# Moving six weight pieces out of attention, four splits from GpSimd to VectorE, and some routing steps, in a three-stage kernel

## The chip, the cores and the metric

The kernel runs on one core of a Trainium2 chip. The metric is the device time of one execution in microseconds (us); lower is better. The engines are called as in the profile: PE is TensorE (matmuls), PEld its weight loads, DVE is VectorE, ACT is ScalarE, POOL is GpSimd, SP is SyncE, which here issues nearly all DMAs.

## The reference

Three stages follow each other on 1536 tokens (2 batches of 768) of 512 values (8 heads of 64).

```python
# 1. attention: keys near the query, and one summary of each block of 32
k_sum, v_sum = k.reshape(.., nb, 32, D).max(3), v.reshape(.., nb, 32, D).mean(3)
a = softmax([where(abs(i - j) < 16, scale * q @ k.T, -1e9), scale * q @ k_sum.T + log(32)])
x = a @ [v, v_sum]                                   # then [1536, 512]
# 2. routed experts: 8 of them, 192 tokens each; pairs (token, expert) are served
#    in the order of falling logits, a full expert takes no more
order = argsort(-(x @ w_gate).flatten())
for tok, e in order:
    if assigned[tok] < 0 and counts[e] < 192:
        assigned[tok] = e
x = relu(x @ w1[e]) @ w2[e]                          # e = assigned[token]
# 3. mixture: every token through 4 domains, 512 -> 1024 -> 512
p = domain_probs / domain_probs.sum(-1)
out = sum(p[:, e] * (relu(x @ v1[e]) @ v2[e]) for e in range(4))
```

The weights are float32. Every large product is made of three half-precision ones: each weight (and each activation) is split into a high half and the rest that the high half leaves.

## The kernel before

**Attention** runs over 24 steps of 128 queries, software-pipelined; `ORDER` lists what a step issues, in the order in which the engines get it. During the later steps `router.first` counts, chunk by chunk, which tokens each expert would take (DVE operations at L521 to L546 of the router, small PE products at L529, L556 and L565). SP's queue carries the loads `kq`, `vb`, `vn` of attention and, between them, weight pieces.

**Weight pieces.** A piece is 128 x 512 float32 (256 KB). It lands in one of a few rotating buffers (`raw`, later also `more`) and is split by `split(hi, lo, r)`: `hi` is the float16 copy, `lo` the difference in bfloat16. `Feed` keeps the pieces in one list: `until(key)` splits all pieces up to a key, `pump` issues as many loads as buffers are free, `next` splits the one that is next if its place is free. Who splits depends on `phase` and on the piece: the first ones of attention are split whole by POOL (L787 and L788), later ones have `hi` on ACT (L790) and `lo` on POOL (L791), and the first four pieces of each routed expert have `lo` on DVE (also L791).

**Pieces within attention.** `hook(i)` is called once in each step and splits the pieces whose entry in the table `HOOK` is this step. Pieces numbered below `POOLHI` go whole to POOL. All 16 pieces of domain 0 and of domain 1 are taken so (32 entries, `w20dt` and `w21dt` in the rows). Pieces of domain 2 (`w2k`, `w2v`) come behind attention: four of them (`NEXT`), then the 16 of the first routed expert (`wp`), then its other twelve, then domain 3 (`w23dt`), then the experts 1 to 7.

**Experts and mixture.** `expert(p)` gives nine jobs: `start` (gathered rows `xg`, which POOL's indirect DMAs at L916 bring, are turned on PE and split by ACT and DVE into `xeh` and `xel`), four `up` jobs (they give `heh`, `hel`) and four `down` jobs (`y0h`, `y0l`). `mixture(t0, nt)` takes `nt` row tiles of 128 tokens through the four domains (`hmh`, `hml`, then `po` and `acc`). `PLAN` says which experts' jobs are slipped into which mixture: expert 0 runs first and alone, expert 1 beside mixture tile 0, experts 2 and 3 beside tiles 1 and 2, experts 4 and 5 beside tiles 3 to 5, experts 6 and 7 beside tiles 6 to 8.

**Routing.** `Router.phases` decides for one expert after another which tokens it takes. It is a generator, a ping-pong of short DVE operations and small PE products (`rt`); each `yield r` names about how long its step takes. A model clock sets where the steps stand in the program: `spend(us)` moves it on by the planned PE work, and `advance` issues the next step and sets when the one behind it is due:

```python
        clock[1] = max(clock[:2]) + SLOW * r + HOP
```

The order on every engine is thus fixed when the program is built; an engine that comes to an instruction whose input is not there waits, and all behind it wait too.

Of the kernel before, what the change touches and what calls it, by code (L numbers as in the profile page):

```python
# [15 lines left out]
OP = mybir.AluOpType  # L16
# [26 lines left out]
class Feed:  # L43
# [16 lines left out]
    def next(self, free):  # L60

        self.pump()
        if self.used in self.held and self.clock[0] >= self.since[self.used] + 3.0 and free(self.used):
            self.jobs[self.used][1](self.held.pop(self.used))
            self.used += 1
            self.pump()
# [10 lines left out]
def three(nc, o, a, b, first, last):  # L77

    for n, (i, j) in enumerate(((0, 0), (0, 1), (1, 0))):
# [8 lines left out]
PLAN = [(0, 1, [1], 26.0, 0.0), (1, 2, [2, 3], 3.0, 7.4), (3, 3, [4, 5], 14.0, 10.6),  # L90
        (6, 3, [6, 7], 2.5, 4.1), (9, 3, [], 0.0, 1.0)]
WB = 5
FEED = [0.96, 0.71, 365.54]
HOOK = [5, 8, 9, 10, 11, 12, 13, 14, 16, 17, 18, 18, 19, 19, 20, 20, 21, 21, 22, 22, 23, 23, 24, 24, 25, 25, 26, 26,
        27, 27, 28, 28]

SOON, NEXT = 0, 4
SCHED = {"prep": [1, 1, 2, 2, 3, 4, 4, 5], "sum": 8, "v": 9, "store": 10, "spread": 11, "kq0": 4, "kq1": 7, "vn": 6}
ORDER = [("pv", 3), ("at", 2), ("r1", 5), ("x", 3), ("r2", 5), ("xt3", 4), ("x2", 3), ("r5", 6), ("at2", 2),
         ("prep", 0), ("r6", 6), ("r3", 5), ("score", 0), ("logit", 4), ("l", 4), ("r0", 4), ("r7", 4), ("r8", 4),  # L100
# [641 lines left out]
def attention_moe_mixture_kernel(  # L742
# [13 lines left out]
    nc = tc.nc  # L756
# [24 lines left out]
    phase = [0]  # L781
    zero = cst.tile([128, 1], F32, name="zero")
    nc.gpsimd.memset(zero, 0.0)

    def split(hi, lo, r, eng=None):
        if phase[0] == 0:
            nc.gpsimd.tensor_tensor(hi, r, zero.to_broadcast([128, PW]), op=OP.add)  # L787
            nc.gpsimd.tensor_tensor(lo, r, hi, op=OP.subtract)  # L788
        else:
            nc.scalar.activation(hi, r, AF.Copy)  # L790
            (eng or nc.gpsimd).tensor_tensor(lo, r, hi, op=OP.subtract)  # L791

    W2 = {}
    feed = Feed(RAW - 1)
# [9 lines left out]
    def add_w2(e, home, js):  # L804

        def load(i):
            r = raw_piece()
            h, c = divmod(i, KD)
            nc.sync.dma_start(r, moe2_w1[e, c * 128:(c + 1) * 128, h * PW:(h + 1) * PW] if h < F // PW
                              else moe2_w2[e, (i - KF) * 128:(i - KF + 1) * 128])  # L810
            return r

        def use(i, r):
            W2[e, i] = home(i)
            split(*W2[e, i], r)

        for i in js:
            feed.add(("w2", e, i), lambda i=i: load(i), lambda r, i=i: use(i, r), lambda: True)

    def kept(pool, e):  # L820
        t = [pool.tile([128, 2 * KF, PW], d, name=f"w2{e}{d}") for d in (F16, BF)]
        return lambda i: [x[:, i] for x in t]

    def reused():

        held = {}

        def part(s, i):
            n = 8 if s == 0 and i >= 8 else 4
            if (s, i // n, n) not in held:  # L830
                d = (F16, BF)[s]
                held[s, i // n, n] = (lod.tile([128, 8, PW], d, name="w2v", tag="vn") if n == 8 else
                                      lod.tile([128, 4, PW], d, name="w2k", tag="kq", bufs=6))
            return held[s, i // n, n][:, i % n]

        return lambda i: [part(s, i) for s in range(2)]

    add_w2(0, kept(cst, 0), range(16))
    add_w2(1, kept(cst, 1), range(16))
    home2 = reused()  # L840
    add_w2(2, home2, range(SOON))

    def hook(i):
        if i == 2:
# [35 lines left out]
        for j in js:  # L880
            feed.add(("p", p, j), lambda j=j: load_piece(p, j), lambda r, j=j: use_piece(p, j, r), lambda: p in EREG)

    add_w2(2, home2, range(SOON, SOON + NEXT))
    add_routed(0, range(16))
    add_w2(2, home2, range(SOON + NEXT, 16))
    add_w2(3, kept(mcst, 3), range(16))
    for p in range(1, E):
        add_routed(p, range(16))
# [35 lines left out]
    def advance():  # L924
        r = next(route, None)
        if r is None:
            clock[1] = 1e9
            return
        if isinstance(r, tuple):
            known[0], r = r  # L930
            when[known[0]] = clock[0]
        clock[1] = max(clock[:2]) + SLOW * r + HOP

    def need(p):
        while known[0] < p:
# [18 lines left out]
    def expert(p):  # L954

        y = [t[:, :, (p % 2) * CAP:(p % 2 + 1) * CAP] for t in YB[p // 2 % 2]]

        def start():
            need(p)
            ready(p, 3)  # L960
            for half in range(2):
                t, p0, n, s0 = place(p, half)
                xg = XG[p, half][p0:p0 + n]
                px = ps.tile([128, KD, 128], F32, name="mm", bufs=3)
                for c in range(KD):
                    nc.tensor.transpose(px[:, c, :n], xg[:, c * 128:(c + 1) * 128], identf[p0:p0 + n, p0:p0 + n])
                parts([x[:, :, s0:s0 + n] for x in XE], px[:, :, :n], SX)
                nc.vector.tensor_copy(PD[p0:p0 + n, t], xg[:, DM:ROW])
            taken.add(p)

        def up(j):
            ready(p, 2 * j + 1)
            ph = ps.tile([128, 2, CAP], F32, name="mm", bufs=3)
            for f in range(2):
                w = [t.rearrange("x (c f) -> x c f", c=KD) for t in WP[p, 2 * j + f]]
                for c in range(KD):
                    three(nc, ph[:, f], [t[:, c] for t in w], [x[:, c] for x in XE], f == 0 and c == 0, c == KD - 1)
            relu([h[:, 2 * j:2 * j + 2] for h in HE], ph)
            eaten[0] += 2

        def down(j):
            ready(p, 2 * j + 9)
            py = ps.tile([128, CAP], F32, name="mm", bufs=3)
            for f in range(KF):
                w = [t[:, f % KD * 128:(f % KD + 1) * 128] for t in WP[p, KF + 2 * j + f // KD]]
                three(nc, py, w, [h[:, f] for h in HE], f == 0, f == KF - 1)
            parts([t[:, j] for t in y], py, SY / SX)
            eaten[0] += 2

        def steady():  # L990
            return known[0] >= p and clock[0] >= when[p] + LATE and feed.used > feed.at["p", p, 3]

        return ([(start, steady)]
                + [(lambda j=j: up(j), lambda: True) for j in range(4)]
                + [(lambda j=j: down(j), lambda: True) for j in range(4)])
# [63 lines left out]
    def spend(us):  # L1059
        clock[0] += us  # L1060
        while clock[2] < clock[0]:
            clock[2] += FEED[clock[0] > FEED[2]]
            feed.next(place_for)
        while clock[1] <= clock[0]:
            advance()

    need(0)
    feed.until(("w2", 2, SOON + NEXT - 1))
    clock[1] = 0.0
    for _ in range(EARLY):  # L1070
        advance()
    for f, _ in expert(0):
        f()
        spend(2.0)
    for t0, nt, side, at, gap in PLAN:
        jobs = [f for p in side for f in expert(p)]
        now = 0.0
        for us in mixture(t0, nt):
            now += us
            spend(us)  # L1080
            while jobs and now >= at and jobs[0][1]():
                jobs.pop(0)[0]()
                spend(2.0)
                at = max(at + gap, now)
        for f, _ in jobs:
            f()
            spend(2.0)


# [25 lines left out]
```

## Time and profile before

| what | value |
|---|---|
| time, median of 3 runs | 880.45 us (877.89 to 886.54) |
| the profiled execution | 886.04 us, of which the span of instructions 884.3 us |
| PE busy | 795.5 us, 90% of the span |
| DVE, ACT, POOL busy | 461.4, 289.2, 259.6 us |
| mean granted clock of TensorE | 0.954 of full speed |
| chain of work that ended last | PE 70%, DVE 18%, DMA 4%, ACT 3%, issue 3%, POOL 2% |

Attention fills the span to about 143 us, expert 0 to about 182 us, the four mixtures with the other experts the rest. In a row of the timeline the first number is the start in us from the start of the span, the second the duration; `x4` says that so many like instructions stand in a row; a bracket tells how long the engine had been idle before and what it waited for.

### The profile page before, as it was taken

What the parts mean: (1) busy time and instruction counts of PE and PEld (TensorE: products, weight loads), DVE (VectorE), ACT (ScalarE), POOL (GpSimd) and SP (SyncE); (2) the same over time, 40 slices, a digit from 0 to 9 for tenths busy, and PEclk for the clock granted to TensorE, in tenths of its full rate; (3) what the DMA queues carried; (4) which work ended last, traced back from release to release, by engine and by line L of the source; (5) the groups of instructions that cost most, each with busy time, mean ns of one, the idle gap of its engine ahead of it and who ended that gap; (6) DMA issues with size and microseconds to landing.
All of it is one profiled execution on the core that took longest, in us unless ns stands there. A gap on an engine that the chain in (4) does not pass through costs nothing.

```text
span 884.3 us, 17221 instructions
## 1 busy us (share of the span) xinstructions
PE 795.5 (90%) x6781; PEld 549.2 (62%) x6822; DVE 461.4 (52%) x1149; ACT 289.2 (33%) x662; POOL 259.6 (29%) x270
## 2 busy tenths in 40 slices
PE   4888984797899999989989999979999999999997
PEld 3776763675596676677555656666666745554553
DVE  6349688667755874766565566675231212321221
ACT  5878784363241222142121312233242201110110
POOL 6457464596150122342112120352313100000001
PEclk9989895699999999989999999999999999999999
DMA  9999664572610610430420220262311000000000
GB/s 196 199 217 246 146 186 146 168 238 78 174 37 13 174 37 14 126 96 1 138 61 13 60 67 25 74 195 67 96 49 36 1 1 18 20 1 1 1 1 36
DMA packets 111536, 76.27 MB, mean 86 GB/s; under 512 B 25440, under 2 KB 98272, under 8 KB 111072
## 3 DMA queue, kind: packets, MB, share of 16 engines
q1 hardware_dynamic: 109472, 68.86, 29.9%
q0 software_dynamic: 1984, 6.32, 2.2%
q8 instruction: 53, 0.87, 0.4%
q14 instruction: 27, 0.22, 0.1%
HBM read 68.77 MB, written 6.42 MB: 85 GB/s over the span
## 4 chain that ended last, share of the span: by engine, by line
PE 70%; DVE 18%; DMA 4%; ACT 3%; issue 3%; POOL 2%; SPq 0%; another core or an unknown queue 0%; POOLq 0%; ACTq 0%; DVEq 0%
PE mm L80 38%; PE po L80 24%; DVE g L602 3%; DMA kq<-in_k_dram 2%; DVE hml L945 1%; DVE wp L791 1%; PE sc L310 1%; DVE ga L540 1%; DVE so L711 1%; PE rt L723 1%; PE rt L596 1%; ACT wp L790 1%; DVE oh L634 1%; ACT kt L264 1%; PE po L346 1%
## 5 line engine op out<-in xcount | busy, mean ns | idle before, releaser
L944 ACT ACTIVATE hmh<-mm 128x384 f16<-128x384 f32 (+2 forms) x160 | 68.3, 427 | 313.7 <-PE mm L80 304.3
L80 PEld LDWEIGHTS <-wp 128*128 128x128 f16 (+1 forms) x1536 | 134.1, 102 | 27.1 <-issue 18.7
L945 DVE SCALAR_TENSOR_TENSOR hml<-mm,hmh 128x384 f16<-128x384 f32 (+2 forms) x160 | 75.3, 475 | 124.2 <-ACT hmh L944 123.8
L80 PEld LDWEIGHTS <-hmh 128*128 128x128 f16 x768 | 73.1, 98 | 77.6 <-issue 0.3
L791 POOL TENSOR_TENSOR wp<-raw,wp 128x512 bf16<-128x512 f32 x54 | 63.3, 1195 | 166.5 <-ACT wp L790 166.4
L602 DVE TENSOR_SCALAR g<-rt,m 128x384 bf16<-128x384 f32 x144 | 79.9, 607 | 1.1 <-PE rt L587 1.1
L80 PE MATMUL mm<-xeh,wp 128*128 128x192 f16 x512 | 76.4, 262 | 2.7 <-ACT xeh L948 1.7
L80 PE MATMUL mm<-xel,wp 128*128 128x192 f16 x256 | 67.2, 262 | 10.7 <-DVE xel L949 10.7
L1047 POOL DMA_INDIRECT out_dram<-acc,ids x12 | 12.2, 1018 | 212.1 <-DVE acc L1031 182.6
L791 POOL TENSOR_TENSOR wp<-more,wp 128x512 bf16<-128x512 f32 x42 | 49.2, 1193 | 83.8 <-ACT wp L790 83.8
L80 PE MATMUL mm<-heh,wp 128*128 128x192 f16 x512 | 70.2, 249 | 0.0
L80 PEld LDWEIGHTS <-hml 128*128 128x128 f16 x384 | 37.6, 98 | 45.5 <-issue 0.3
L80 PE MATMUL mm<-hel,wp 128*128 128x192 f16 x256 | 63.8, 249 | 0.0
L1031 DVE SCALAR_TENSOR_TENSOR acc<-po,pn,acc 128x512 f32<-128x512 f32 x36 | 25.7, 744 | 72.2 <-PE po L80 72.1
L945 DVE SCALAR_TENSOR_TENSOR hel<-mm,heh 128x384 f16<-128x384 f32 x32 | 17.8, 557 | 75.2 <-ACT heh L944 75.2
L80 PEld LDWEIGHTS <-w2k 128*128 128x128 f16 (+1 forms) x480 | 43.3, 100 | 19.7 <-issue 0.5
L944 ACT ACTIVATE heh<-mm 128x384 f16<-128x384 f32 x32 | 15.7, 491 | 100.0 <-PE mm L80 98.5
L916 POOL DMA_INDIRECT xg<-xd,idx x16 | 16.1, 1006 | 92.1 <-DVE m L732 64.2
L790 ACT ACTIVATE wp<-more 128x512 f16<-128x512 f32 x64 | 37.0, 622 | 6.7 <-DMA more<-in_moe_w_dram 6.5
L80 PEld LDWEIGHTS <-w23dt.float 128*128 128x128 f16 x320 | 29.3, 98 | 14.3 <-issue 1.3
L80 PEld LDWEIGHTS <-w20dt.float 128*128 128x128 f16 x320 | 29.4, 98 | 13.1 <-issue 0.7
L790 ACT ACTIVATE wp<-raw 128x512 f16<-128x512 f32 x64 | 36.9, 621 | 1.9 <-DMA raw<-in_moe_w_dram 1.9
(251 smaller groups left out, 1944.5 us busy)
## 6 DMA issues: line engine op xcount, KB each, us to landing
raw<-in_moe_w_dram SPq DMA_DIRECT2D x112, 256.0 KB
more<-in_moe_w_dram SPq DMA_DIRECT2D x80, 256.0 KB
vb<-in_v_dram SPq DMA_DIRECT2D x16, 240.0 KB
kq<-in_k_dram SPq DMA_DIRECT2D x8, 384.0 KB
kq<-in_q_dram SPq DMA_DIRECT2D x8, 384.0 KB
vn<-in_v_dram SPq DMA_DIRECT2D x4, 768.0 KB
xd<-x SPq DMA_DIRECT2D x48, 64.0 KB
vb<-vsum_d SPq DMA_DIRECT2D x4, 292.5 KB
```

The source lines that it names most:

```text
L80: nc.tensor.matmul(o, a[i], b[j], start=first and n == 0, stop=last and n == 2, skip_group_check=True)
L264: nc.scalar.activation(o[:, :, :, :, r], pt[r * 64:r * 64 + 64].rearrange("x j (c i) -> x c i j", i=R), AF.Copy, scale=scale)
L310: nc.tensor.matmul(sc[:, t, p], QT[Q][:, p, 2 * ch + t], KT[Q][:, p, 2 * ch + t], start=False, stop=True, skip_group_check=True)
L346: nc.tensor.matmul(po[s, 2 * t + p], AT[u][:, 2 * t + p, s], VB[Q][:, 2 * ch + t, 2 * hh + p], start=True, stop=True)
L602: nc.vector.tensor_scalar(g[:, c - c0], row, m[:, 0, c:c + 1], None, op0=OP.is_le)
L790: nc.scalar.activation(hi, r, AF.Copy)
L791: (eng or nc.gpsimd).tensor_tensor(lo, r, hi, op=OP.subtract)
L916: nc.gpsimd.indirect_dma_start(out=XG[p, half][p0:p0 + n], out_offset=None, in_=xd[:, :], in_offset=bass.IndirectOffsetOnAxis(ap=idx[half] ...
L944: nc.scalar.activation(h[0], p, AF.Relu)
L945: nc.vector.scalar_tensor_tensor(h[1], p, 0.0, h[0], op0=OP.max, op1=OP.subtract)
L1031: nc.vector.scalar_tensor_tensor(acc[i], po[i], s, acc[i], op0=OP.mult, op1=OP.add)
L1047: nc.gpsimd.indirect_dma_start(out=out[:, :], out_offset=bass.IndirectOffsetOnAxis(ap=IDS[:, t0 + i:t0 + i + 1], axis=0), in_=acc[i], in_o ...
```

## The change

Four things change. `HOOK` loses six entries, at the early steps, and the entries that stay are renumbered, so that the last six pieces of domain 1 leave attention; `POOLHI` goes from 10 to 4. Behind attention now come four pieces of domain 1, the 16 of expert 0, the last two of domain 1, and all 16 of domain 2. For the four pieces directly behind attention (`phase` 2) the `lo` half isn't issued at once: it is kept in `later` and issued on DVE behind expert 0's `start`. In the loop over `PLAN`, `begin()` may issue the `start` of the second of two experts before the last four jobs of the first. And `SLOW`, the factor on the routing steps' lengths, becomes a tuple: 1.0 as before for the experts 0 to 3, 1.3 from expert 4 on.

```diff
-SLOW, HOP = 1.0, 0.3
+SLOW, HOP = (1.0, 1.0, 1.0, 1.0, 1.3), 0.3
-POOLHI = 10
+POOLHI = 4
-HOOK = [5, 8, 9, 10, 11, 12, 13, 14, 16, 17, 18, 18, 19, 19, 20, 20, 21, 21, 22, 22, 23, 23, 24, 24, 25, 25, 26, 26,
-        27, 27, 28, 28]
+HOOK = [10, 13, 15, 17, 18, 18, 19, 19, 20, 20, 21, 21, 22, 22, 23, 23, 24, 24, 25, 25, 26, 26, 27, 27, 28, 28]
...
+    later = []
     def split(hi, lo, r, eng=None):
...
             nc.scalar.activation(hi, r, AF.Copy)
-            (eng or nc.gpsimd).tensor_tensor(lo, r, hi, op=OP.subtract)
+            if phase[0] == 2:
+                later.append(lambda: nc.vector.tensor_tensor(lo, r, hi, op=OP.subtract))
+            else:
+                (eng or nc.gpsimd).tensor_tensor(lo, r, hi, op=OP.subtract)
...
-    add_w2(2, home2, range(SOON, SOON + NEXT))
+    add_w2(1, home1, range(len(HOOK) - 16, len(HOOK) - 16 + NEXT))
     add_routed(0, range(16))
-    add_w2(2, home2, range(SOON + NEXT, 16))
+    add_w2(1, home1, range(len(HOOK) - 16 + NEXT, 16))
+    add_w2(2, reused(), range(16))
...
-        clock[1] = max(clock[:2]) + SLOW * r + HOP
+        clock[1] = max(clock[:2]) + SLOW[min(known[0] + 1, len(SLOW) - 1)] * r + HOP
...
-    feed.until(("w2", 2, SOON + NEXT - 1))
+    phase[0] = 2
+    feed.until(("w2", 1, len(HOOK) - 16 + NEXT - 1))
+    phase[0] = 1
...
-    for f, _ in expert(0):
+    for n, (f, _) in enumerate(expert(0)):
         f()
+        if n == 0:
+            for g in later:
+                g()
         spend(2.0)
...
+        def begin():
+            n = next((n for n, (f, _) in enumerate(jobs) if f.__name__ == "start"), 0)
+            if 0 < n <= 4 and jobs[n][1]():
+                jobs.pop(n)[0]()
```

In the changed program the lines behind `split` stand four lines lower (L791 is L793 and L795 there, L949 is L953), those of the router one line higher (L634 is L633).

**POOL around the first gather** (`xg<-xd,idx` at L916). Before:

```order
L791 TENSOR_TENSOR w20dt.bfloat_107<-raw,w20dt.float_106 128x512 x6
L791 TENSOR_TENSOR w21dt.bfloat_109<-raw,w21dt.float_108 128x512 x16
L916 DMA xg<-xd,idx 128x516
L916 DMA xg<-xd,idx 64x516
L791 TENSOR_TENSOR w2k<-more,w2k 128x512 x3
L791 TENSOR_TENSOR w2k<-raw,w2k 128x512
L791 TENSOR_TENSOR wp_2420<-more,wp_2419 128x512
```

After:

```order
L795 TENSOR_TENSOR w20dt.bfloat_107<-raw,w20dt.float_106 128x512 x12
L795 TENSOR_TENSOR w21dt.bfloat_109<-raw,w21dt.float_108 128x512 x10
L920 DMA xg<-xd,idx 128x516
L920 DMA xg<-xd,idx 64x516
L795 TENSOR_TENSOR wp_2394<-more,wp_2393 128x512
L795 TENSOR_TENSOR wp_2400<-raw,wp_2399 128x512
```

The splits of the pieces that leave attention no longer stand ahead of the gather, and behind the gather the four `w2k` splits are gone: POOL's next work is that of expert 0's later pieces.

**DVE in the same place**, from the operation at L634 that marks the chosen expert up to expert 0's first `hel`. Before:

```order
L634 TENSOR_TENSOR oh<-lm,m 128x96
L635 TENSOR_TENSOR ohb<-oh,alive 128x96
L791 TENSOR_TENSOR wp_2353<-raw,wp_2352 128x512
L791 TENSOR_TENSOR wp_2359<-raw,wp_2358 128x512
L791 TENSOR_TENSOR wp_2365<-raw,wp_2364 128x512
L791 TENSOR_TENSOR wp_2371<-more,wp_2370 128x512
L949 SCALAR_TENSOR_TENSOR xel<-mm,xeh 128x4x128
L968 COPY pd<-xg 128x4
L949 SCALAR_TENSOR_TENSOR xel<-mm,xeh 128x4x64
L968 COPY pd<-xg 64x4
L945 SCALAR_TENSOR_TENSOR hel<-mm,heh 128x384
```

After:

```order
L633 TENSOR_TENSOR oh<-lm,m 128x96
L634 TENSOR_TENSOR ohb<-oh,alive 128x96
L795 TENSOR_TENSOR wp_2323<-raw,wp_2322 128x512
L795 TENSOR_TENSOR wp_2329<-more,wp_2328 128x512
L795 TENSOR_TENSOR wp_2335<-more,wp_2334 128x512
L795 TENSOR_TENSOR wp_2341<-more,wp_2340 128x512
L953 SCALAR_TENSOR_TENSOR xel<-mm,xeh 128x4x128
L972 COPY pd<-xg 128x4
L953 SCALAR_TENSOR_TENSOR xel<-mm,xeh 128x4x64
L972 COPY pd<-xg 64x4
L793 TENSOR_TENSOR w21dt.bfloat_109<-more,w21dt.float_108 128x512
L793 TENSOR_TENSOR w21dt.bfloat_109<-raw,w21dt.float_108 128x512 x3
```

The four `lo` halves (L793) stand on DVE behind the second `xel`, ahead of the first `hel`; ahead of `xel` nothing changed.

**DVE in the routing for expert 6**, beside expert 5, where the operations from `four<-rt` to the cast `above` (L658 to L667) lead to a PE product that waits for `above`. Before:

```order
L652 TENSOR_REDUCE four<-four 128x1
L1031 SCALAR_TENSOR_TENSOR acc<-po,pn,acc 128x512
L658 TENSOR_REDUCE four<-rt 128x1
L659 TENSOR_SCALAR m<-m,four 128x12
L660 TENSOR_SCALAR m<-m,four 128x12
L662 TENSOR_TENSOR oh<-ohb,m 128x96
L663 TENSOR_TENSOR lm<-ohb,m 128x96
L665 TENSOR_REDUCE four<-lm 128x8
L667 CAST above<-four 128x8
L1031 SCALAR_TENSOR_TENSOR acc<-po,pn,acc 128x512
L673 TENSOR_TENSOR lm<-rt,remx 128x96
```

After:

```order
L651 TENSOR_REDUCE four<-four 128x1
L949 SCALAR_TENSOR_TENSOR hel<-mm,heh 128x384 x3
L657 TENSOR_REDUCE four<-rt 128x1
L658 TENSOR_SCALAR m<-m,four 128x12
L659 TENSOR_SCALAR m<-m,four 128x12
L661 TENSOR_TENSOR oh<-ohb,m 128x96
L662 TENSOR_TENSOR lm<-ohb,m 128x96
L664 TENSOR_REDUCE four<-lm 128x8
L666 CAST above<-four 128x8
L953 SCALAR_TENSOR_TENSOR y0l<-mm,y0h 128x192 x3
L672 TENSOR_TENSOR lm<-rt,remx 128x96
```

The same operations stand later: before, between two `acc` of the mixture's end, ahead of expert 5's `xel`; now behind expert 5's `hel`, ahead of its `y0l`.

## Rows read from the trace of the kernel before

**Rows 1.** The page: busy time of PE; the granted clock in 40 slices.

```profile
PE 795.5 (90%) x6781; PEld 549.2 (62%) x6822; DVE 461.4 (52%) x1149; ACT 289.2 (33%) x662; POOL 259.6 (29%) x270
...
PEclk9989895699999999989999999999999999999999
```

**Rows 2.** Windows: length, busy PE, PEld, DVE, ACT, POOL; clock; DMA share; GB/s.

```profile
40.00:60.00 20.00, 16.26 (x182) 13.72 (x181) 7.83 (x23) 15.75 (x43) 6.20 (x10) 0.89 0.98 219
60.00:80.00 20.00, 19.24 (x240) 16.28 (x240) 16.69 (x52) 16.49 (x47) 14.55 (x18) 0.94 0.99 224
...
190.00:194.00 4.00, 4.00 (x36) 2.03 (x35) 4.00 (x10) 3.14 (x6) 4.00 (x5) 1.00 0.78 240
...
589.00:592.00 3.00, 3.00 (x32) 2.86 (x30) 0.38 (x2) 0.28 (x2) 0.00 (x0) 0.62 0.84 244
```

**Rows 3.** Timeline, attention, SP's queue and then PE.

```profile
46.91 0.43 SPq L809 DMA_DIRECT2D raw<-in_moe_w_dram  x1
...
49.11 0.54 SPq L144 DMA_DIRECT2D kq<-in_k_dram  x1
...
57.18 0.88 PE L261 MATMUL tp<-identf,kq 96*128 96x96 f32 x4 [3.62 <-DMA kq<-in_k_dram]
```

**Rows 4.** Timeline, attention, 79 to 98 us: POOL, DVE and PE.

```profile
79.80 5.69 POOL L185 TENSOR_TENSOR vn<-vn 96x1024 f32<-96x1024 f32 x5 [0.50 <-DMA vn<-in_v_dram]
...
79.93 2.38 DVE L535 SCALAR_TENSOR_TENSOR ge<-rows,m,before 128x128 bf16<-128x128 f32 x1
...
85.10 0.32 PE L529 MATMUL misc<-identf,m 128*128 128x128 f32 x1 [3.31 <-DVE m L521]
...
95.44 1.66 DVE L546 TENSOR_TENSOR ga<-rows,m 128x640 bf16<-128x640 f32 x1
...
97.16 0.29 PE L565 MATMUL cnt<-oh,ga 128*128 128x8 bf16 x5 [1.27 <-DVE ga L546]
```

**Rows 5.** Timeline, the first gather: POOL, DVE, ACT, PE; one DVE row from later.

```profile
153.74 3.38 POOL L791 TENSOR_TENSOR w2k<-more,w2k 128x512 bf16<-128x512 f32 x3
...
153.43 4.92 DVE L634 TENSOR_TENSOR oh<-lm,m 128x96 bf16<-128x96 f32 x1
...
442.74 0.26 DVE L634 TENSOR_TENSOR oh<-lm,m 128x96 bf16<-128x96 f32 x1
...
158.56 1.88 DVE L791 TENSOR_TENSOR wp<-raw,wp 128x512 bf16<-128x512 f32 x3
...
156.06 1.03 ACT L948 ACTIVATE xeh<-mm 128x512 f16<-128x512 f32 x2 [2.21 <-PE mm L966]
...
162.11 0.32 PE L80 MATMUL mm<-xel,wp 128*128 128x192 f16 x1 [4.65 <-DVE xel L949]
```

**Rows 6.** Timeline, mixture tile 0 and, last, the end of tiles 3 to 5: DVE.

```profile
199.52 4.15 DVE L650 SCALAR_TENSOR_TENSOR four<-n,four 128x4 f32<-128x4 f32 x1
...
205.84 1.23 DVE L659 TENSOR_SCALAR m<-m,four 128x12 f32<-128x12 f32 x1
...
209.30 1.20 DVE L663 TENSOR_TENSOR lm<-ohb,m 128x96 f32<-128x96 bf16 x1
...
554.68 0.25 DVE L659 TENSOR_SCALAR m<-m,four 128x12 f32<-128x12 f32 x1
```

**Rows 7.** Waits of PE, 449 to 560 us: us in total, times, longest.

```profile
PE rt L596 <- DVE g L602: 1.8, 3, 1.4
PE rt L655 <- DVE four L652: 1.1, 2, 0.7
```

**Rows 8.** Timeline, expert 5 and the start of expert 6: POOL, PE.

```profile
569.91 2.98 POOL L791 TENSOR_TENSOR wp<-raw,wp 128x512 bf16<-128x512 f32 x2 [1.08 <-ACT wp L790]
...
578.74 4.52 POOL L791 TENSOR_TENSOR wp<-raw,wp 128x512 bf16<-128x512 f32 x4
...
587.84 0.23 PE L686 MATMUL rt<-ohb,ones 128*128 128x96 bf16 x1 [4.65 <-DVE ohb L635]
...
598.44 0.46 PE L966 MATMUL mm<-identf,xg 64*128 64x64 f32 x4 [2.07 <-DVE hml L945]
```

More of the change, by code (lines that the diff above doesn't have):

```diff
@@ L93 @@
 FEED = [0.96, 0.71, 365.54]
-HOOK = [5, 8, 9, 10, 11, 12, 13, 14, 16, 17, 18, 18, 19, 19, 20, 20, 21, 21, 22, 22, 23, 23, 24, 24, 25, 25, 26, 26,
-        27, 27, 28, 28]
-SOON, NEXT = 0, 4
+HOOK = [10, 13, 15, 17, 18, 18, 19, 19, 20, 20, 21, 21, 22, 22, 23, 23, 24, 24, 25, 25, 26, 26, 27, 27, 28, 28]
+NEXT = 4
 SCHED = {"prep": [1, 1, 2, 2, 3, 4, 4, 5], "sum": 8, "v": 9, "store": 10, "spread": 11, "kq0": 4, "kq1": 7, "vn": 6}
@@ L838, in attention_moe_mixture_kernel @@
     add_w2(0, kept(cst, 0), range(16))
-    add_w2(1, kept(cst, 1), range(16))
-    home2 = reused()
-    add_w2(2, home2, range(SOON))
+    home1 = kept(cst, 1)
+    add_w2(1, home1, range(len(HOOK) - 16))
     def hook(i):
@@ L1071, in attention_moe_mixture_kernel @@
         advance()
-    for f, _ in expert(0):
+    for n, (f, _) in enumerate(expert(0)):
         f()
+        if n == 0:
+            for g in later:
+                g()
         spend(2.0)
     for t0, nt, side, at, gap in PLAN:
-        jobs = [f for p in side for f in expert(p)]
+        jobs = [job for p in side for job in expert(p)]
+        def begin():
+            n = next((n for n, (f, _) in enumerate(jobs) if f.__name__ == "start"), 0)
+            if 0 < n <= 4 and jobs[n][1]():
+                jobs.pop(n)[0]()
         now = 0.0
@@ L1080, in attention_moe_mixture_kernel @@
             spend(us)
+            begin()
             while jobs and now >= at and jobs[0][1]():
@@ L1084, in attention_moe_mixture_kernel @@
                 at = max(at + gap, now)
-        for f, _ in jobs:
-            f()
+        while jobs:
+            begin()
+            jobs.pop(0)[0]()
             spend(2.0)
```

## The prediction

> **What bounds the kernel now.** I read the page first: PE is busy for 795.5 us, 90% of the span, and its 549.2 us of weight loads run beside that [rows 1]. The change leaves the number of matmuls as it is, so it can only touch the 89 us in which PE idles (884.3 − 795.5), or what PE loses to its clock; the clock slices show where that was low, above all in slices 7 and 8, 132 to 177 us [rows 1]. So I next read PE's waits in order of time, took those over 0.5 us, and asked in the timeline of the engine named what held it. Four places bear on the change: the middle of attention, the first gather, mixture tile 0, and the routing of experts 4 to 7.
>
> In attention the DMA engines are full: share 0.98 and 0.99 between 40 and 80 us, at 219 and 224 GB/s [rows 2]. PE waits there for loads and, from 80 us on, for the router's DVE work, which is slow beside POOL [rows 3, 4]. At the first gather DVE's operation at L634 takes 4.92 us, where the same one takes 0.26 us later, with POOL idle; it ends as POOL's four `w2k` splits end, and PE waits 4.65 us for the `xel` behind it [rows 5]. This is the plainest case in the trace of what splits on POOL cost.
>
> **Part one, six pieces leave attention.** Each takes 256 KB from the DMA queues and two POOL operations (or one on ACT and one on POOL) from the steps between 45 and 98 us. Three waits bear on it.
>
> The wait for `kq` at 57.18 us, 3.62 us long: its transfer was issued at 49.11 us, behind a weight piece issued at 46.91 us that is now gone [rows 3]. At 219 GB/s a piece is 1.20 us of transfer; where weights flow alone, 240 GB/s at a share of 0.78, a full share would do it in 0.85 us [rows 2]. I take 1.0.
>
> The wait for `m` at 85.10 us, 3.31 us: DVE's count operations at 79.93 us and behind it run beside POOL's five sums of `vn`, 5.69 us from 79.80 us on, and the first takes 2.38 us. Those sums waited 0.50 us for their transfer, which shared the queue with weight pieces [rows 4]. They come earlier by that and a little; I take 0.8, since the sums stay and DVE still meets them.
>
> The wait for `ga` at 97.16 us, 1.27 us: the operation took 1.66 us while POOL split a piece whole [rows 4]. Two such pieces stood there; in the new table one is left in that step. I take 1.1, and 0.1 for what is left.
>
> Sum: −3.0. The bounds are 0 (the next wait takes each place: PE is bound by DVE and ACT in this stretch as well) and −8.2 (3.62 + 3.31 + 1.27, all gone). From step 18 on the table is the same, two pieces to a step, so nothing changes there.
>
> **Part two, the first gather.** Four POOL splits go, 3.38 us for three of them and as much again for a fourth by the mean, 4.5 us in all [rows 5]. Then L634 takes some 0.3 instead of 4.92 us, DVE's splits of expert 0's own pieces (1.88 us for three) are through 4.6 us earlier, and what is late next is ACT, whose two `xeh` end at 157.09 us [rows 5]. PE's product with `xel` can start some 0.9 us behind that, at 158.0 instead of 162.11: −4.1. Against it: the four pieces keep their buffers until DVE has split them, so expert 0's next loads go out some 3 us later. They land ahead of use by a little; I put 0.3 on it. The four deferred DVE operations, four at 0.63 (1.88/3), are 2.5 us, and stand ahead of the first `hel`. They are covered by expert 0's first up job, whose 24 products run at half clock right after the start; without that cover they would cost up to 2.5. I take **−3.8**, between −1.6 and −4.6.
>
> **Part three, mixture tile 0.** Behind expert 0's pieces now come 34 of the domains instead of 28, all with `lo` on POOL: 6 x 1.13 (3.38/3, [rows 5]) = 6.8 us more. POOL isn't waited for directly, but DVE beside it is slow: L650 takes 4.15 us at 199.52, L659 1.23 us, which with POOL idle is 0.25 us [rows 6]. These stay. What is new is that the block of splits ends some 6 us later, so one or two more routing operations fall beside it. One at the price of L659 costs 1.0 and is covered in part; one at the price of L650 costs 4. I take +0.5, between 0 and +4.
>
> GPSIMD Engine Reference, a page of the Trainium skill, says in section 8, Key points, that GpSimd contends with VectorE instructions in a two-port mode or with two SBUF inputs. The trace bears that out for L634, which has two tensors as inputs, and leaves L659 open, which has one tensor and a column; by a reading in which L659 isn't touched, the next part would be 1.9 us cheaper (two such operations at 0.25 instead of 1.2) and the time 871 us. The row shows L659 five times slower beside POOL, so the sum goes by the row.
>
> **Part four, `begin()`.** It moves nothing. Its condition asks that the fourth weight piece of the second expert has been split, and the places for it come free only two at a time as the first expert's jobs are done; with the call left out the order is the same, row for row, on all five engines. The title's third part therefore costs and gives nothing. It stands here as a rival that is settled: that the change doesn't do what it says.
>
> **Part five, routing from expert 4 on comes later.** This alone moves PE and DVE instructions behind expert 2. For the better: between 449 and 560 us PE waited 1.8 us at L596 and 1.1 us at L655 for DVE's answers, 2.9 us in these two rows [rows 7]; a step that stands 1.3 times as far from the last one leaves DVE longer, and I expect 0.9 to be left, −2.0. For the worse: what is left of the routing for experts 6 and 7 then falls beside expert 5. Before, PE waited 4.65 us there for `ohb` (expert 7's choice) and 2.07 us for `hml` at expert 6's start [rows 8], and ran at clock 0.62 behind the first of these [rows 2]. After, `above` for expert 6 stands behind three `hel` of expert 5, beside the twelve splits on POOL that in the trace run from 569.91 us to 583.26 us without a break [rows 8]. Four operations at 1.2 instead of 0.25 us [rows 6] are 3.8 us more, of which an up job's end covers about one: a wait of 2.7. The wait for `ohb` falls from 4.65 to some 2.4, since expert 5's work lies closer behind it, and that at expert 6's start moves to `xel`, 1.4 for 2.07. With a second stretch at low clock, 1.0 more, that is 2.7 − 2.25 − 0.67 + 1.0 = +0.8, rounded to +1.0. Together **−1.0**, from −5 (both halves good) to +10 (below).
>
> **The sum.** −3.0 − 3.8 + 0.5 − 1.0 = −7.3. The profiled execution took 886.04 us, so it would take 878.7; it was a long one of its kind, 5.6 us over the median of the three runs. All parts are differences of waits, so I take them off the median: 880.45 − 7.3 = **873.1 us**.
>
> **The rivals.**
>
> *More is gained.* Attention's three waits go whole (−8.2) or the late routing stops waiting (−5). One of them gives 4 to 5 us more: 868 to 869, and both 864. For it: the DMA engines are full and everything behind them queues. Against: in attention DVE and ACT are busy for 16 of 20 us between 60 and 80 us [rows 2], so a wait gone brings the next.
>
> *Less is gained.* Attention's relief is hidden behind the next wait (0 for −3.0) and the late routing gives nothing back (+1 for −1): 878; with tile 0 at its bound as well, 881. Only the first gather is then left.
>
> *It ends slower.* One mechanism: DVE's first operation of expert 6's `above` is held not for 1.2 us but until POOL's run of splits ends, as L634 and L650 were held until theirs did [rows 5, 6]. Before, that run had four pieces in a row; beside expert 5 it has twelve, 13.4 us [rows 8]. PE covers some 2 to 4 us with the job in hand and then stands: 9.4 to 11.4 us, and a low clock of 1 to 2 us behind it. In place of −1.0 the late routing is then +9.4 to +12, and the total +3 to +6: 883.5 to 886.5; if expert 7's choice is held in the same way, another 5. It decides against the change from 6.3 us of new waiting on, which is what the other parts give (3.0 + 3.8 − 0.5). For it: two operations of the trace were held just so. Against: in tile 0 the operations from L659 to L663 stood beside splits and took 1.2 us each, not the whole block [rows 6], and the splits come one by one as ACT gives them.
>
> **How the numbers follow.** The forecast's own case, 869 to 877, gets 0.55; more gained, 860 to 869, 0.15; less gained, 877 to 883, 0.22; slower, 883 to 892, 0.08. The range 862 to 884 leaves out about 0.04 below and 0.07 above. What a measurement of this kernel can tell from no change is about 1%, 8.8 us: below 871.6 counts as faster, above 889.3 as slower. Of the first case 0.28 lies below 871.6, with the second 0.43. Of the last case 0.03 lies above 889.3. So faster 0.43, within 1% 0.54, slower 0.03.
>
> **What would show each step.** Right, if in the changed profile: DVE's L633 at the first gather takes under 0.5 us, PE's wait for `xel` there is under 1 us and the four L793 stand under expert 0's first products; `kq` at 57 us is waited for by a us less and the waits at 85 and 97 us are shorter; tile 0's two waits behind L650 and L663 look as before; PE's waits for routing between 449 and 560 us sum to 1 us; and beside expert 5 the new wait is at `above`, 2 to 3 us. Wrong, if the first gather's wait only moves to expert 0's second pair of pieces (loads too late), if the waits in attention keep their size, or if PE stands over 5 us beside expert 5 with DVE's L658 held beside POOL.

## The result, and the profile after

The changed kernel takes 871.12 us (median of 15 runs, 866.45 to 877.16), the kernel before 881.62 (15 runs, 877.89 to 888.21): a ratio of 0.9865, 95% interval 0.9835 to 0.9895. The forecast was 873.1 us, off the then known median of 880.45: −7.3 us, where −10.5 came. The profiled execution of the changed kernel took 871.12 us, span 869.3, against 886.04 and 884.3.

The page of the changed kernel, busy times and the clock in 40 slices:

```profile
PE 790.5 (91%) x6782; PEld 545.7 (63%) x6822; DVE 456.6 (53%) x1153; ACT 291.1 (33%) x668; POOL 248.9 (29%) x260
...
PEclk9999995999999999999999999999999999999999
```

Beside [rows 1]: PE's busy time fell by 5.0 us with the same matmuls, and its idle time from 88.8 (884.3 − 795.5) to 78.8 us. So a third of the 15 us between the two profiles isn't waiting that went, but the same matmuls done in less busy time; the mean granted clock rose from 0.954 to 0.966, and one low slice is left where there were two. The 15 us are more than the 10.5 between the medians, since the profiled execution of the kernel before is 4.4 us over its median and that of the changed kernel at its median.

To see where the time went I took, from the timelines, the start of the first PE instruction of each stage; a stage's length is the distance to the next one. The first stage holds attention and the routing for expert 0; the last ends where the mixture of tiles 9 to 11 begins, which takes 130.5 to 130.9 us in every kernel. This is done for every kernel that follows, since one stage's length is compared better than a whole time:

| kernel | to the routing for expert 1 | first gather, expert 0 | tile 0, expert 1 | tiles 1, 2, experts 2, 3 | tiles 3 to 8, experts 4 to 7 |
|---|---|---|---|---|---|
| before | 152.3 | 30.0 | 79.6 | 142.3 | 349.6 |
| after | 145.5 | 24.8 | 79.3 | 142.1 | 346.8 |

Attention gave 6.8 us, the first gather 5.2, the late routing 2.8, and the two stages between nothing to speak of.

**The first gather.** The timeline of the changed kernel, DVE and then PE:

```profile
146.60 0.26 DVE L633 TENSOR_TENSOR oh<-lm,m 128x96 bf16<-128x96 f32 x1
...
147.67 1.89 DVE L795 TENSOR_TENSOR wp<-more,wp 128x512 bf16<-128x512 f32 x3
149.91 0.69 DVE L953 SCALAR_TENSOR_TENSOR xel<-mm,xeh 128x512 f16<-128x512 f32 x1 [0.35 <-ACT xeh L952]
...
151.59 1.88 DVE L793 TENSOR_TENSOR w21dt.bfloat<-raw,w21dt.float 128x512 bf16<-128x512 f32 x3
155.39 0.56 DVE L949 SCALAR_TENSOR_TENSOR hel<-mm,heh 128x384 f16<-128x384 f32 x1 [1.92 <-ACT heh L948]
...
151.06 0.32 PE L80 MATMUL mm<-xel,wp 128*128 128x192 f16 x1 [0.41 <-DVE xel L953]
```

The operation that took 4.92 us [rows 5] takes 0.26. DVE is through with expert 0's own pieces before ACT has `xeh`; DVE waits 0.35 us for ACT, and PE 0.41 us in place of 4.65. The four deferred splits end at 153.5 us, and DVE then idles for 1.92 us until ACT gives `heh`: they cost nothing.

**Attention.** PE's waits in the timeline of the changed kernel, the longer ones up to 95 us:

```profile
55.55 0.80 PE L260 MATMUL tp<-identf,kq 96*128 96x96 f32 x4 [2.39 <-DMA kq<-in_k_dram]
...
80.54 0.52 PE L260 MATMUL tp<-identf,kq 96*128 96x96 f32 x4 [1.14 <-ACT rows L530]
84.81 0.32 PE L528 MATMUL misc<-identf,m 128*128 128x128 f32 x1 [0.79 <-DVE m L520]
91.31 0.28 PE L564 MATMUL cnt<-oh,ga 128*128 128x8 bf16 x5 [1.39 <-DVE ga L545]
```

The wait for `kq` went from 3.62 [rows 3] to 2.39 us. That for `m` went from 3.31 [rows 4] to 0.79, with a new one of 1.14 for ACT just ahead of it. The first stage as a whole, of the kernel before and then of the changed one (columns as in [rows 2]):

```profile
0.00:152.32 152.32, 113.19 (x1292) 94.31 (x1292) 103.47 (x262) 107.92 (x268) 84.35 (x115) 0.86 0.85 192
```

```profile
0.00:145.49 145.49, 110.34 (x1292) 91.90 (x1292) 99.28 (x262) 107.81 (x268) 70.98 (x103) 0.90 0.83 190
```

PE idles for 39.1 us (152.32 − 113.19) before and 35.1 after, and its 1292 matmuls are done in 2.9 us less of busy time. Windows of 20 us show the clock beside that, first of the kernel before, then of the changed one:

```profile
80.00:100.00 20.00, 14.59 (x168) 12.41 (x167) 17.60 (x36) 13.03 (x35) 13.48 (x14) 0.82 0.91 181
100.00:120.00 20.00, 19.77 (x231) 16.16 (x229) 11.65 (x36) 16.33 (x44) 12.07 (x11) 0.92 0.66 172
```

```profile
60.00:80.00 20.00, 18.84 (x239) 15.91 (x237) 17.31 (x58) 18.04 (x50) 6.87 (x11) 1.00 0.93 214
80.00:100.00 20.00, 17.15 (x216) 14.90 (x217) 15.59 (x35) 15.25 (x41) 12.25 (x15) 0.91 0.83 165
100.00:120.00 20.00, 17.54 (x232) 13.98 (x231) 14.92 (x44) 17.99 (x51) 13.79 (x12) 1.00 0.71 186
```

Between 60 and 120 us the clock was 0.94, 0.82 and 0.92 and is 1.00, 0.91 and 1.00: 20 x (0.06 + 0.09 + 0.08) = 4.6 us of full clock more, part of which falls into waits.

**Tile 0.** DVE and PE in the timeline of the changed kernel:

```profile
187.58 4.13 DVE L649 SCALAR_TENSOR_TENSOR four<-n,four 128x4 f32<-128x4 f32 x1
...
194.52 1.22 DVE L658 TENSOR_SCALAR m<-m,four 128x12 f32<-128x12 f32 x1
...
200.28 0.22 PE L669 MATMUL rt<-above,ones 128*128 128x96 bf16 x1 [1.72 <-DVE above L666]
216.21 1.00 PE L722 MATMUL rt<-tok,so 128*128 128x1 f16 x28 [0.72 <-DVE so L710]
```

The first two are L650 and L659 of [rows 6], held as there: 4.13 us for 4.15, 1.22 for 1.23. PE's wait for `above` is 1.72 us for 2.7. One wait is new, 0.72 us behind `so`; it stands in all nine kernels, this one and those of the experiments, that have 34 pieces there, and in none of the four with 28.

**The late routing.** All of PE's waits behind tile 2, in the changed kernel:

```profile
PE rt L685 <- DVE ohb L634: 3.3, 1, 3.3
PE mm L80 <- DVE xel L953: 2.7, 3, 1.6
PE rt L669 <- DVE above L666: 2.4, 1, 2.4
PE mm L80 <- ACT xeh L952: 1.3, 3, 0.6
PE rt L586 <- DVE top L626: 1.2, 1, 1.2
PE rt L586 <- DVE four L646: 0.7, 1, 0.7
PE rt L595 <- DVE g L601: 0.3, 1, 0.3
```

They sum to 11.9 us; the same view of before gives 14.3, led by the 4.65 for `ohb` [rows 8]. The waits of [rows 7] are down to 0.3 and 0, the new one at `above` is 2.4. POOL's splits, and then what DVE did beside them ahead of `above`:

```profile
557.59 4.50 POOL L795 TENSOR_TENSOR wp<-more,wp 128x512 bf16<-128x512 f32 x4
562.06 4.53 POOL L795 TENSOR_TENSOR wp<-raw,wp 128x512 bf16<-128x512 f32 x4
566.55 1.15 POOL L795 TENSOR_TENSOR wp<-more,wp 128x512 bf16<-128x512 f32 x1
...
561.63 0.50 DVE L658 TENSOR_SCALAR m<-m,four 128x12 f32<-128x12 f32 x1
562.04 1.20 DVE L659 TENSOR_SCALAR m<-m,four 128x12 f32<-128x12 f32 x1
563.28 1.17 DVE L661 TENSOR_TENSOR oh<-ohb,m 128x96 bf16<-128x96 bf16 x1
564.37 1.20 DVE L662 TENSOR_TENSOR lm<-ohb,m 128x96 f32<-128x96 bf16 x1
```

Each took at most about as long as one split of POOL (4.53/4 = 1.13 us); none was held to the end of the run at 567.70 us.

### The profile page after: what moved, and what is told of

The parts are those of the page before. It is cut to its first block, busy times and chain, and to the rows that moved or that the text cites. A ratio compares the mean times of both kernels' runs of the same rounds, so it can differ in the third digit from the quotient of the medians.

```text
span 869.3 us, 17212 instructions
## 1 busy us (share of the span) xinstructions
PE 790.5 (91%) x6782; PEld 545.7 (63%) x6822; DVE 456.6 (53%) x1153; ACT 291.1 (33%) x668; POOL 248.9 (29%) x260
## 4 chain that ended last, share of the span: by engine, by line
PE 71%; DVE 17%; ACT 4%; DMA 4%; issue 3%; POOL 1%; SPq 0%; POOLq 0%; ACTq 0%; DVEq 0%
PE mm L80 38%; PE po L80 25%; DVE g L601 2%; DMA kq<-in_k_dram 2%; PE sc L309 1%; DVE so L710 1%; DVE hml L949 1%; DVE wp L795 1%; DVE ga L539 1%; ACT kt L263 1%; PE ta L329 1%; PE rt L595 1%; PE rt L722 1%; PE po L345 1%; ACT qt L263 1%
## 5 line engine op out<-in xcount | busy, mean ns | idle before, releaser
L949 DVE SCALAR_TENSOR_TENSOR hml<-mm,hmh 128x384 f16<-128x384 f32 (+2 forms) x160 | 75.3, 475 | 126.0 <-ACT hmh L948 125.7
L80 PEld LDWEIGHTS <-hmh 128*128 128x128 f16 x768 | 73.6, 99 | 78.9 <-issue 1.3
L795 POOL TENSOR_TENSOR wp<-raw,wp 128x512 bf16<-128x512 f32 x56 | 67.7, 1230 | 133.6 <-ACT wp L791 132.2
L80 PE MATMUL mm<-xeh,wp 128*128 128x192 f16 x512 | 74.2, 258 | 3.4 <-ACT xeh L952 3.2
L795 POOL TENSOR_TENSOR wp<-more,wp 128x512 bf16<-128x512 f32 x40 | 45.4, 1156 | 84.2 <-ACT wp L791 84.2
L949 DVE SCALAR_TENSOR_TENSOR hel<-mm,heh 128x384 f16<-128x384 f32 x32 | 17.8, 558 | 63.1 <-ACT heh L948 63.0
L80 PEld LDWEIGHTS <-w23dt.float 128*128 128x128 f16 x320 | 29.5, 98 | 14.4 <-issue 1.3
L80 PEld LDWEIGHTS <-w21dt.float 128*128 128x128 f16 x320 | 30.0, 99 | 12.6
L791 ACT ACTIVATE wp<-more 128x512 f16<-128x512 f32 x64 | 37.0, 622 | 1.3 <-DMA more<-in_moe_w_dram 1.1
L80 PE MATMUL po<-w23dt.float,hml 128*128 128x512 f16 x96 | 36.9, 384 | 0.6 <-issue 0.2
```

The lines of the kernel that those rows point to most:

```text
L80: nc.tensor.matmul(o, a[i], b[j], start=first and n == 0, stop=last and n == 2, skip_group_check=True)
L949: nc.vector.scalar_tensor_tensor(h[1], p, 0.0, h[0], op0=OP.max, op1=OP.subtract)
```

## The experiments

All are timed against the kernel before on the same chip, five rounds each; its medians there were 883.4 to 883.7 us. Ratios are to it, with the 95% interval. Three chips were used, and the changed kernel's 871.12 us was measured beside a kernel before of 881.62, so a difference of 1 or 2 us from it tells nothing. The question: which part gave what, and what in attention.

**Transfers alone back in attention.**

```diff
+        if i in (6, 9, 10, 12, 13, 15):        # in hook(i), ahead of feed.pump()
+            nc.sync.dma_start(d, moe2_w1[2, :128, :PW])     # d: a free part of w21
```

> The changed kernel with six transfers of 256 KB issued again at the steps 6, 9, 10, 12, 13 and 15 of attention, into places that are written again later; no split of them. The two profiles show PE 6.6 us ahead at the end of attention. If the DMA queue was what the six pieces cost, most of it comes back: 4 to 6 us over the changed kernel, PE's wait for kq near 57 us at 3.6 us again. If POOL was the cost, the time stays within 1.5 us of the changed kernel (871) and only the wait for kq grows, by about 1 us.

871.1 us, 0.9869 (0.983 to 0.9908): no loss that can be seen. In its profile the routing for expert 1 starts at 148.0 us, 2.5 later than in the changed kernel, and between 40 and 143 us PE waits 5.5 us for `kq` in three waits, none over 3.0, where the changed kernel waits 2.4 in one.

**Splits alone back in attention.**

```diff
+        if i in (5, 8, 9, 11, 12, 14):         # in hook(i)
+            nc.gpsimd.tensor_tensor(dh, dr, zero.unsqueeze(1).to_broadcast([128, 4, 128]), op=OP.add)
+            nc.gpsimd.tensor_tensor(dl, dr, dh, op=OP.subtract)     # dr: identf, four times
```

> The changed kernel with six whole splits on POOL (two operations each, of a tile that lies in SBUF already) at the steps 5, 8, 9, 11, 12 and 14; no transfer. If POOL beside the router's DVE work was the cost, 3 to 5 us over the changed kernel, with PE waiting over 2 us again for DVE's m near 85 us. If the DMA queue was the cost, within 1.5 us of it. If both share it, this and the run with the transfers alone each give 2 to 3.5 us.

872.04 us, 0.9877 (0.9832 to 0.9922). PE waits 3.1 us for `m` in five waits, none over 1.2, where one of over 2 us was expected. By the times neither of the two alone is the 6 us. The trace says otherwise of this one: it reaches the routing for expert 1 at 149.8 us, 4.3 later than the changed kernel.

**Factor 1.0 for all experts.**

```diff
-SLOW, HOP = (1.0, 1.0, 1.0, 1.0, 1.3), 0.3
+SLOW, HOP = (1.0, 1.0, 1.0, 1.0, 1.0), 0.3
```

> The changed kernel with the routing steps at the factor 1.0 for all experts, as before. By the sum of the prediction it is 1.0 us slower than the changed kernel; by the shift between the two profiles from expert 3 on, 2.9 us. If later routing only moves waits from one place to another, the same within 0.5 us. Up to the middle of the span the trace is that of the changed kernel.

872.86 us, 0.9888 (0.9849 to 0.9927). Tiles 3 to 8 take 349.5 us, as before the change, with the same waits as there, 14.3 us in all.

**No deferral.**

```diff
-    phase[0] = 2
+    phase[0] = 1
     feed.until(("w2", 1, len(HOOK) - 16 + NEXT - 1))
```

> The changed kernel with the four lo halves on POOL behind the first gather again, in place of DVE behind expert 0's start. By the prediction 3.8 us slower: DVE's L633 at the first gather takes over 4 us and PE waits 4.6 us for xel. If what was late was rather the weights or ACT, within 1 us of the changed kernel.

872.43 us, 0.9881 (0.9842 to 0.992): by the medians only 1.3 us slower, where 3.8 were expected. Its trace shows the old wait whole, first DVE and then PE:

```profile
144.86 4.92 DVE L633 TENSOR_TENSOR oh<-lm,m 128x96 bf16<-128x96 f32 x1
...
153.53 0.32 PE L80 MATMUL mm<-xel,wp 128*128 128x192 f16 x1 [4.68 <-DVE xel L953]
```

The stage takes 29.2 us for 24.8. The profiled execution wasn't longer by that, since its attention was 1.8 us shorter and the two stages behind the first gather 0.9. That much is scatter: the five kernels with this order in attention reach the routing for expert 1 at 143.3 to 145.5 us, and the control below takes 1.7 us less in tiles 1 and 2 with the changed kernel's order.

**Attention as before, all behind it as after.** The ten early entries are back, six of them with pieces that are loaded and split to places written again later.

```diff
+OLD = [5, 8, 9, 10, 11, 12, 13, 14, 16, 17]
+FAKE = (0, 1, 2, 4, 5, 7)          # of these ten, the six that the change took out
+    steps, keys, real = OLD + HOOK[4:], [], 0     # hook(i) goes by steps; POOLHI = 10
...
```

> The changed kernel with six pieces more in attention, at the steps and in the order of the kernel before: each is loaded and then split whole by POOL, so that POOL waits for the transfer; their halves go to places that are written again later. Attention then issues what the kernel before issues, all behind it is the changed kernel's. The transfers alone gave 871.1 and the splits alone 872.0 us. If the two cost only together (POOL, and what is queued behind it there, waits for a piece that lands late), about 877 us, PE 5 to 7 us later at the end of attention, and POOL shows waits for raw of over 1 us. If attention's 6.6 us between the two profiles were chance of those two executions, within 2 us of the changed kernel.

877.43 us, 0.9933 (0.9899 to 0.9966): 5.7 to 6.3 us of the change's gain are gone (against the control below and the changed kernel). The profiled execution, 873.77 us, was a short one. POOL's waits from 20 to 100 us, this kernel:

```profile
POOL w21dt.float L790 <- DMA raw<-in_moe_w_dram: 3.5, 1, 3.5
POOL w20dt.float L790 <- DMA raw<-in_moe_w_dram: 2.0, 1, 2.0
```

In the changed kernel POOL doesn't wait for a piece's transfer in this stretch (it waits 7.1 us for ACT's halves of pieces), nor in the two runs with transfers or splits alone; in the kernel before it waits 4.4 us in two.

**Only the pieces moved.** The kernel before with the change's table and order of pieces, without deferral and with factor 1.0; the edit is to the changed kernel.

```diff
-    phase[0] = 2
+    phase[0] = 1
-SLOW, HOP = (1.0, 1.0, 1.0, 1.0, 1.3), 0.3
+SLOW, HOP = (1.0, 1.0, 1.0, 1.0, 1.0), 0.3
```

> The kernel before with only the pieces moved: the short table, domain 1's last six pieces behind attention, but the four lo halves on POOL and the routing factor at 1.0. By the traces' shifts 6 to 7 us faster than before, 1% of it left out by tile 0: ratio about 0.993. If attention's gain was chance, ratio 0.998 or more. If the parts only gain together, over 0.996 with the first gather unchanged.

877.88 us, 0.9935 (0.9905 to 0.9965), with its routing for expert 1 at 145.5 us, like the changed kernel's.

**All but the moved pieces.** Deferral and factor in the kernel before.

```diff
-            (eng or nc.gpsimd).tensor_tensor(lo, r, hi, op=OP.subtract)
+            if phase[0] == 2:
+                later.append(lambda: nc.vector.tensor_tensor(lo, r, hi, op=OP.subtract))
...
-SLOW, HOP = 1.0, 0.3
+SLOW, HOP = (1.0, 1.0, 1.0, 1.0, 1.3), 0.3
```

> The kernel before with its own table of pieces, the four lo halves on DVE behind expert 0's start and the routing factor 1.3 from expert 4 on: the whole change but for the moved pieces. By the prediction's sum 4.8 us faster than before, by the traces' shifts 7 us: ratio 0.992 to 0.9945. If the gain is attention's alone, ratio 0.998 or more.

878.74 us, 0.994 (0.9918 to 0.9963), inside what was expected.

**The control, without begin().**

```diff
-            if 0 < n <= 4 and jobs[n][1]():
+            if False and jobs[n][1]():
```

> The changed kernel without the call of begin. The order of instructions is the same on all engines, so the time is the changed kernel's, 871 us, to within what runs of one program differ: medians of six runs within 2 us, and single profiles that differ by up to 3 us in attention.

871.78 us, 0.9874 (0.9843 to 0.9905): the same time from the same order.

**Transfers and splits, not linked.** The edits of the first two experiments together.

> The changed kernel with the six transfers and the six whole splits on POOL at the early steps, but not linked: the transfers go to places that no split reads, and the splits read a tile that lies in SBUF. Alone the transfers gave 871.1 us and the splits 872.0, both linked as in the kernel before 877.4. If POOL's waits for late pieces are what costs (in the linked run it stood 3.5 and 2.0 us for them), this stays at 871 to 873.5 us. If transfers and splits only cost together because the queue and POOL are then both full, 875 to 878 us.

873.85 us, 0.9893 (0.9863 to 0.9924): 3.6 us under the linked run, 2.1 to 2.7 over the changed kernel and its control, and between the two expectations. The trace reaches the routing for expert 1 at 147.5 us, 2.1 before the linked run's.

**The factor alone, in the kernel before.**

```diff
-SLOW, HOP = 1.0, 0.3
+SLOW, HOP = (1.0, 1.0, 1.0, 1.0, 1.3), 0.3
```

> The kernel before with the routing factor 1.3 from expert 4 on, nothing else. By the prediction 1.0 us faster than before (ratio 0.999), by the run of the changed kernel at factor 1.0 1.7 us (0.998), by the shifts between profiles 3 to 4 us (0.996). If its gain needed the other parts, 1.0.

877.68 us, 0.9942 (0.9916 to 0.9967): 5.7 us, a larger gain than any that was expected. Tiles 3 to 8 take 346.8 us for 349.6, and PE's waits there are those of the changed kernel, each to 0.1 us.

**The deferral alone, in the kernel before.** The edit of "All but the moved pieces" without its factor.

> The kernel before with only the four lo halves behind the first gather on DVE, behind expert 0's start. By the prediction 3.8 us faster (ratio 0.9957), by the shift of the profiles at the first gather 4.3 to 5.6 us (0.994 to 0.995). If part of it is given back later, as the small loss of the changed kernel without it hints, 1 to 2 us (0.998).

878.37 us, 0.9938 (0.9909 to 0.9968). The stage of the first gather takes 25.3 us for 30.0. Tiles 3 to 8 take 353.6 us; PE idles there as in the kernel before (15.1 us for 15.5), but is busy for 4.4 us longer, at a clock of 0.98 for 0.99.

**All early pieces out.**

```diff
-POOLHI = 4
+POOLHI = 0
-HOOK = [10, 13, 15, 17, 18, 18, 19, 19, 20, 20, 21, 21, 22, 22, 23, 23, 24, 24, 25, 25, 26, 26, 27, 27, 28, 28]
+HOOK = [18, 18, 19, 19, 20, 20, 21, 21, 22, 22, 23, 23, 24, 24, 25, 25, 26, 26, 27, 27, 28, 28]
```

> The changed kernel with the four early pieces that are left (steps 10, 13, 15 and 17) also moved behind attention, so that POOL splits no piece whole and ten pieces of domain 1 wait. If early pieces cost what the six did, about 1 us each, 867 to 869 us. If POOL no longer waits for a piece in the changed kernel, they cost little: 870 to 872. If the ten pieces come late for the first mixture tile, PE waits for w21 between 185 and 215 us and it is slower than the changed kernel, 873 to 877.

870.59 us, 0.9843 (0.9809 to 0.9878): the fastest median, but its interval holds the changed kernel's 0.9865. By the medians the early pieces that are left cost little, as the second expectation had it. It reaches the routing for expert 1 at 142.6 us; PE waits for no piece of `w21`. Tile 0 takes 82.2 us there, with the clock at 0.58 from 216 to 220 us and 0.70 from 228 to 232 us.

**All stages together** (us, from the profiled execution of each):

| kernel | attention | first gather | tile 0 | tiles 1, 2 | tiles 3 to 8 |
|---|---|---|---|---|---|
| factor alone | 151.8 | 29.3 | 76.5 | 142.2 | 346.8 |
| deferral alone | 150.5 | 25.3 | 76.5 | 141.9 | 353.6 |
| both | 155.3 | 24.4 | 78.8 | 142.1 | 346.8 |
| pieces alone | 145.5 | 29.6 | 79.0 | 142.4 | 349.6 |
| after, attention as before | 149.6 | 24.9 | 79.7 | 140.4 | 346.9 |
| after, transfers back | 148.0 | 25.3 | 78.8 | 140.4 | 346.8 |
| after, splits back | 149.8 | 24.4 | 78.1 | 141.5 | 346.8 |
| after, both unlinked | 147.5 | 24.3 | 78.1 | 141.4 | 346.9 |
| after, factor 1.0 | 143.3 | 24.3 | 77.9 | 142.1 | 349.5 |
| after, no deferral | 143.7 | 29.2 | 78.9 | 141.6 | 346.8 |
| after, no begin | 145.4 | 25.5 | 78.8 | 140.4 | 346.7 |
| after, all early out | 142.6 | 24.5 | 82.2 | 142.2 | 346.9 |

The last column splits cleanly by the factor: 346.7 to 346.9 with 1.3, 349.5 to 349.6 with 1.0, but for one run at 353.6. So does the first gather by the deferral: 24.3 to 25.5 with it, 29.2 to 30.0 without. Attention scatters: 143.3 to 145.5 us in the five kernels with the new order, 150.5 to 155.3 in the four with the old one.

## Why the prediction was right

The forecast of 873.1 us, its direction and its range held. That 873.1 lies within 2.0 us of the 871.12 is in part luck: the gain was 3.2 us larger than forecast, and the kernel before came out 1.2 us slower than its first three runs had shown it. By the steps of the forecast:

- **Attention, −3.0 forecast.** This term was mis-sized: the old table's five profiles reach the routing for expert 1 at 149.6 to 155.3 us (mean 151.9), the five of the new one without added work at 143.3 to 145.5 (mean 144.7), −7.2; by the times it is 5.7 (pieces alone) to 6.3 (attention back). The three waits did shrink about as forecast: `kq` by 1.23 (1.0), `m` by 2.52 less a new wait of 1.14, so 1.4 (0.8), the two for `ga` from 1.98 to 1.39, 0.6 (1.1). That is 3.2 us. Single waits are no safe sign, though: in the control, with the changed kernel's order, `m` costs 2.46 us at 80 us, and at 55 us PE waits 1.07 us for ACT instead of the transfer of `kq`. The sum of a stage is steadier: PE's idle time in it is 36.0 to 40.0 us (mean 38.9) with the old order and 33.0 to 35.1 (mean 34.1) with the new one, and its busy time 113.0 and 110.6 in the mean. So 4.8 of the 7.2 us are waits, more than the three that were priced, and 2.4 are the same matmuls done in less time. The sum left out both: further waits, and PE's speed. The clock, which goes into that speed (in this stage 0.85 to 0.89 in the mean with the old order, 0.86 to 0.90 with the new one), had been named at the prediction's head as one of two things that the change can touch, and was then priced beside expert 5 but not here.
- **What in the six pieces costs** was taken as transfers for one wait and POOL for the others, added up. By the medians transfers alone cost 0 and splits alone 0.9 us, together 2.1 to 2.7, and linked, a split waiting for its own late transfer with POOL's sums of `vn` queued behind it, 5.7 to 6.3. That POOL waits for a piece's transfer in the five kernels with the old table (4.4 to 6.1 us) and in none of the others is shown. That these waits are the 3.6 us between linked and unlinked is not: the runs of the two overlap (872.6 to 882.3 and 870.4 to 877.7), and the traces disagree. By PE's idle time in the stage the linked run stands out (39.4 us, where unlinked has 36.4, splits alone 36.5 and transfers alone 35.4); by the stage's length it doesn't (149.6, where they have 147.5, 149.8 and 148.0). What in the six pieces costs stays open.
- **The first gather, −3.8.** Right in mechanism, low by 1: the stage is 4.7 us shorter (means of 24.8 and 29.5). For expert 0's pieces, whose later loads were to cost 0.3, PE waits 0.20 us at most, and the stage's mean clock is 0.82 for 0.74. The times give 1.3 us (taken out of the changed kernel) and 5.0 (put into the one before).
- **Tile 0, +0.5.** Within the scatter: 76.5 to 79.6 us with 28 pieces, 77.9 to 79.7 with 34, and one new wait of 0.72 us.
- **begin(), nothing:** 871.78 against 871.12 us. It is the third part of the change, not of the title as the prediction has it.
- **The late routing, −1.0.** It gave 2.8. The better half came as forecast, −2.0: the waits at L595, L654, L586 and L574 sum to 2.2 us (0.3, none, 0.7 and 1.2, none), where the same view of before has 4.2 (2.1, 1.3, 0.5, 0.3). The worse half, +0.8 by its terms and +1.0 in the sum, was a gain of about 0.8, as the rest of the 2.8 says: `above` costs 2.4 (2.7 forecast) and `ohb` 3.3 for 4.65 (2.4), but expert 6's start shows 0.57 and 0.61 us (1.4) where two waits of 2.6 in all for `hml` went, and the second stretch at low clock, priced at 1.0, didn't come: beside expert 5 there is one in either kernel, behind `ohb` before (0.62 from 589 to 592 us) and behind `above` now (0.50 from 568 to 571 us). Waits explain 0.4 of this 0.8 (2.4 of the 2.8, 14.3 less 11.9); the rest stays open.
- **The slower rival** fell: L658 to L662 took 0.5 to 1.2 us each beside POOL's splits. But L649 was held for 4.13 us in tile 0 again, and no run tells which of the two happens to an operation. (The rival's price was added loosely: 9.4 to 11.4 and 1 to 2 us make 10.4 to 13.4, not 9.4 to 12.) The rule of GPSIMD Engine Reference in the Trainium skill (section 8, Key points), read so that L659 stays untouched for its one input tensor, doesn't hold: the same operation, now L658, took 1.22 us in tile 0 again. The rule itself isn't contradicted by that, since it names a two-port mode beside the two inputs, and no run shows whether this operation uses one.

What stays open: the three parts alone give 5.7, 5.7 and 5.0 us, deferral and factor together 4.8, all together 10.5 to 11.8. By stages the parts are 7.2, 4.7 and 2.8, which is 14.7 us less what tile 0 takes, and so 3 to 4 more than the times show. Some 2 us of that come from which executions were profiled: those of the five kernels with the old order in attention lie 1.2 us above their medians on average, those of the five with the new one 1.0 below. Medians of 6 to 12 runs of a kernel whose runs differ by 5 to 12 us carry 2 to 4 us of uncertainty each, by the intervals, so the runs don't settle whether the parts overlap.

## What to carry to other kernels

When a piece of work is taken out of a busy stage, price the stage's whole idle time and PE's busy time, and not only the waits that stand out: here three named waits gave 3.2 us, all waits 4.8, and the same matmuls in less time another 2.4. When several edits of 3 to 5 us are to be told apart and runs scatter by 10, compare stage lengths in the traces: here they told two of the three parts apart to within a microsecond, which the medians could not. For the third, attention, one profile of each kernel was too few: its length scatters by 2 to 5 us.

## What was not expected of the hardware

The clock fell behind a wait in one execution and not behind the same wait in another. The changed kernel and its control have the same instructions in the same order, and in both PE waits 1.23 us for `so` at 347 us. Windows behind that wait, of the changed kernel and then of the control:

```profile
347.00:350.00 3.00, 2.86 (x41) 2.32 (x42) 0.42 (x2) 0.18 (x1) 0.00 (x0) 0.87 0.30 87
350.00:353.00 3.00, 2.78 (x8) 1.14 (x8) 2.48 (x17) 0.21 (x1) 1.71 (x2) 0.57 0.14 37
```

```profile
347.00:350.00 3.00, 2.70 (x42) 2.35 (x44) 0.52 (x2) 0.30 (x1) 0.00 (x0) 1.00 0.36 89
350.00:353.00 3.00, 3.00 (x22) 1.82 (x22) 2.60 (x17) 0.08 (x1) 1.83 (x2) 1.00 0.14 44
```

The clock falls to 0.57 in the one and stays at 1.00 in the other, and the stage takes 142.1 and 140.4 us. What made it fall in the one isn't shown. Differences of this size stand in other stages of the table above too, and some of the scatter between runs of one kernel is likely made of them; that part is argued, not shown.
